# Asking for some first-batch loads in pieces with 1024-byte packets

## The chip, the cores and the metric

The kernel runs on one core of one Trainium2 chip. The metric is the device time of one execution in microseconds (us), lower is better. The engines named below are PE (TensorE, the matmuls), DVE (VectorE), ACT (ScalarE), POOL (GpSimd) and SP (SyncE, which here only issues transfers). Transfers of all issuing engines run on the same 16 DMA engines.

## The reference

There are 8 batches of 3008 rows. Each goes through a gated attention without softmax and then through an MLP mixer over rows (tokens) and over columns (channels). Cut to what is computed:

```python
# u, v: (8, 3008, 256); z: (8, 3008, 64); all float32
scores = (1 / S) * z @ z^T                 # S = 3008
out    = maximum(scores, 0)**2 @ v
x      = u * out                           # the gate
h      = maximum(x^T @ w_tok1, 0) @ w_tok2 # w_tok1 (3008, 256), w_tok2 (256, 3008)
u2     = x + h^T
result = u2 + maximum(u2 @ w_ch1, 0) @ w_ch2   # w_ch1 (256, 1536), w_ch2 (1536, 256)
```

## The kernel before, in words

**Tiling.** The 3008 rows of a batch are cut into six groups of 512 (the last has 448). A group is four tiles of 128 rows (`GK = 4`); the last has three and a tail of 64 rows. `b` counts batches, `q` a group of queries, `g` a group of keys. For each (b, q) the scores with every key group go to PSUM (line 440), ACT takes the relu (L478, L466), DVE squares it (L486, L518), and PE multiplies it with v (L593 in the very first block, L677 elsewhere). At the end of a block, `gate` (L835, and L840 for the odd 64 columns) multiplies the sum with the transposed u, `uT`, on DVE. The gated x goes through a DMA transpose (`turn_x`, L855) to `x_sb`. When all six groups of a batch are there, the mixer of this batch runs: first token product (L900), second (L927), first channel product (L977), second channel product (L1096, in a form with seven products for eight, which uses the precomputed weight sums `w_sums`, L1616 to L1619 on DVE).

**Order of the work.** The program that builds the kernel holds a small model of the engines with costs in us. It decides in which order the pieces are written to each engine's queue (`next_op`, `next_piece`, the main loop at the end). Each engine executes its queue strictly in that order and waits on semaphores where data are missing. A load tells this model its cost through `loading(LOAD)`.

**Loads.** All float32 inputs except the first z are loaded by POOL with a cast to bf16 on the way. `load_v` (L211, and L214 for the tail), `load_u` (L223, L226), `load_w_tok1` (L241, L245), `load_w_tok2` (L251) and `load_w_ch` (L258 for the first channel weight in two parts, L263 for the second in two parts) each issue one transfer per group or part. `rows_of` lays a group out so that a partition takes n consecutive rows (n = 4, or 3 in the last group): for v, u and w_tok1 a partition's piece in SBUF is 4 x 256 bf16 = 2048 bytes, or 1536 in the last group; for a part of w_ch1 it is 1536 bf16 = 3072 bytes; for w_tok2 it is 512 bf16 = 1024 bytes.

In batch 0 POOL is asked for: v of batch 0; u of groups 0 to 3 of batch 0; z of batch 1; and then the list `items`, spread over the steps of batch 0: v of batch 1, w_tok1, w_tok2, w_ch1 and w_ch2, u of the first two groups of batch 1; u of groups 4 and 5 of batch 0 come in between. Nothing but free buffers and the transfers' own semaphores holds POOL back in this stretch. These semaphores are eight lanes used in turn: each POOL transfer waits until the one eight before it has landed, so at most eight are in flight. A group of u is named by m = 6 b + q below.

**Transposes.** SP issues, in one queue, the DMA transposes of u (`turn_u`, L233), of z for the next batch (`turn_z`, L140 and L144), of x (L855), of squared scores that serve a mirrored block (`flip`, L546 and L530), of u2 (L958), and the stores of the result (L1151). An SP transfer that waits, or that cannot be handed over, holds back all behind it.

Of the kernel before, what the change touches and what calls it, by code (L numbers as in the profile page):

```python
# [13 lines left out]
P = 128  # L14
QW = 512
GK = 4
# [41 lines left out]
def kernel(  # L58
# [11 lines left out]
    nc = tc.nc  # L70
# [3 lines left out]
    d_ch = moe_w_ch1.shape[-1]  # L74
# [6 lines left out]
    NQ = (S + QW - 1) // QW  # L81
# [16 lines left out]
    w_tok1_sb = consts.tile([P, KT, d_tok], BF16)  # L98
    w_tok2_sb = consts.tile([P, DT, S], BF16)
    w_ch1_sb = consts.tile([P, DT, d_ch], BF16)  # L100
# [12 lines left out]
    def rows_of(ap, c):  # L113

        n = full_tiles[c]
        return ap[c * QW:c * QW + n * P, :].rearrange("(p t) d -> p t d", t=n)

    def last_rows(ap):
        return ap[(KT - 1) * P:, :]
# [75 lines left out]
    def fill(n, bank):  # L195

        for _ in range(n):
            nc.tensor.matmul(  # L198
                bank, zero[:, :P], zero[:], start=True, stop=True, skip_group_check=True)

    def load_v(b, c):
        if b == 0:

            vt = sb.tile([P, GK, D], BF16, tag="fl", name="v_sb", bufs=ROOM["fl"])
            live["fl"] += 1
            fl_free.pop(0)
        else:
            vt = sb.tile([P, GK, D], BF16, tag="v", name="v_sb", bufs=ROOM["v"])
            live["v"] += 1
        n = full_tiles[c]  # L210
        nc.gpsimd.dma_start(out=vt[:, :n, :], in_=rows_of(v[b], c))  # L211
        if n < GK:
            for r in range(2):
                nc.gpsimd.dma_start(  # L214
                    out=vt[r * TAIL:(r + 1) * TAIL, n, :], in_=last_rows(v[b]))
        vs[b, c] = vt
        v_in[b, c] = Done(pe[0] + 9.0 if b > 1 else 0.0)
        loading(LOAD)

    def load_u(b, q):  # L220
        ur = sb.tile([P, QW // P, D], BF16, tag="ur", name="ur", bufs=4)
        n = full_tiles[q]
        nc.gpsimd.dma_start(out=ur[:, :n, :], in_=rows_of(u[b], q))  # L223
        if n < QW // P:
            nc.gpsimd.memset(ur[TAIL:, n, :], 0.0)
            nc.gpsimd.dma_start(out=ur[:TAIL, n, :], in_=last_rows(u[b]))  # L226
        urs[b, q] = ur
        loading(LOAD)
# [9 lines left out]

    def load_w_tok1(c):
        n = full_tiles[c]  # L240
        nc.gpsimd.dma_start(  # L241
            out=w_tok1_sb[:, c * GK:c * GK + n, :], in_=rows_of(moe_w_tok1, c))
        if n < GK:
            nc.gpsimd.memset(w_tok1_sb[TAIL:, KT - 1, :], 0.0)
            nc.gpsimd.dma_start(  # L245
                out=w_tok1_sb[:TAIL, KT - 1, :], in_=last_rows(moe_w_tok1))
        loading(LOAD)
# [7 lines left out]

    def load_w_ch(part):
        if part < 2:
            nc.gpsimd.dma_start(  # L258
                out=w_ch1_sb[:, part, :], in_=moe_w_ch1[part * P:(part + 1) * P, :])
        else:  # L260
            h = CHT // 2
            c0 = (part - 2) * h
            nc.gpsimd.dma_start(  # L263
                out=w_ch2_sb[:, c0:c0 + h, :],
                in_=moe_w_ch2.rearrange("(cc c) d -> c cc d", c=P)[:, c0:c0 + h, :])
        loading(LOAD * 1.5)
# [46 lines left out]
    def loading(us):  # L313
        loads[0] = max(loads[0], pe[0] + 1.0) + us
# [96 lines left out]
    def can_score(first_unit, most):  # L411

        n, at = 0, live["at"]
        for (b, q, g), pr in units[first_unit:first_unit + most]:
            if (b, q) not in turned or (b, g) not in turned:
                break
            at += pr == 0
            if at > ROOM["at"]:
                break
            n += 1  # L420
        return n
# [1038 lines left out]
    make_identity(nc, ident)  # L1460
    zf0 = [first_z(c) for c in range(NG)]
    load_v(0, 0)
    nc.gpsimd.memset(zs[:, 0, :], 0.0)
    nc.gpsimd.memset(zs[:, KT + 1, :], 0.0)
# [41 lines left out]
    def u_then_turn(m):  # L1506
        load_u(m // NQ, m % NQ)
        later.append((pe[0] + 11.0, lambda: gated[0] >= m - 2,
                      lambda: turn_u(m // NQ, m % NQ)))
# [6 lines left out]
    def when_taken(b, c):  # L1516
        ask(lambda: load_v(b + 1, c),
            lambda: x_done[b, NQ - 1].t is not None and has_room(("v",)))
# [13 lines left out]
    for b in range(B):  # L1532
        base = b * NQ * NG
        for q in range(NQ):
            m = b * NQ + q + 2
            if b == 0:
                if m < NQ:
                    at_group(U_LOADS[m], lambda m=m: load_u(m // NQ, m % NQ))
                late_turn = NQ * NG + 1 + 4 * (m - NQ) if m >= NQ else U_TURNS[m]
                at_group(base + late_turn, lambda m=m: turn_u(m // NQ, m % NQ))  # L1540
            elif m < 2 * NQ:
                at_group(base + q * NG + 2, lambda m=m: ask(lambda: u_then_turn(m)))
        if b == 0:
            at_group(base + 4, lambda b=b: new_zT(b + 1))
            for j in range(NG):
                at_group(base + 4 + j // 3, lambda b=b, j=j: load_z(b + 1, j))
            for half in range(2):
                at_group(base + 9 + 6 * half, lambda b=b, half=half: turn_next_z(b, half))
        else:
            if b == 1:  # L1550
                ask_z(2, base + NG - 1)
            if b + 1 < B:
                last, m = base + NQ * NG - 1, (b + 1) * NQ
                for k in range(3):
                    ask_u(m + k, last)
                if b + 2 < B:
                    ask_z(b + 2, last)
                for c in vorder:
                    at_group(last, lambda b=b, c=c: when_taken(b, c))
                for k in range(3, NQ):  # L1560
                    ask_u(m + k, last)
# [45 lines left out]
    def ask_w_ch(part):  # L1607
        load_w_ch(part)
        w_done[part].t = pe[0] + 16.0
        if part == 3:  # L1610
            push("dve", pe[0] + 18.0, 2.4, 2.5, sum_weights, done=sums_done)
# [12 lines left out]
    def ask_w_tok2(c):  # L1624
        load_w_tok2(c)
        tok2_done[c].t = pe[0] + 10.0

    items = [lambda c=c: load_v(1, c) for c in vorder]
    items += [lambda c=c: load_w_tok1(c) for c in range(NG)]
    items += [lambda c=c: ask_w_tok2(c) for c in range(NG)]  # L1630
    items += [lambda part=part: ask_w_ch(part) for part in range(4)]
    items += [lambda m=m: load_u(m // NQ, m % NQ) for m in (NQ, NQ + 1)]
    for k, item in enumerate(items):
        at_group(NG + 1 + k * (NQ * NG - 2 * NG + W_LATER) // len(items), item)
# [39 lines left out]
    while cur[0] is not None or heads or tails:  # L1674
        run_engines(pe[0])
        ask_some()
        t = pe[0]
# [16 lines left out]
        n = can_score(done_units, most)  # L1694
# [118 lines left out]
```

## Time and profile before

| what | us |
|---|---|
| time, median of 3 runs | 1117.28 (1116.62 to 1120.8) |
| the profiled execution's own time | 1116.15 |
| its span in the profile | 1114.4 |
| PE busy in the span | 1104.5 (99%) |
| DVE busy | 760.5 (68%) |
| ACT busy | 670.5 (60%) |
| POOL busy | 150.6 (14%) |
| packets of POOL's transfers (queue q0) | 27344 packets, 32.32 MB |
| packets of SP's and ACT's transfers (queue q1) | 445024 packets, 131.57 MB |

Busy times are unions of an engine's instructions. Issuing a transfer is not counted as busy. The profiled execution's own time is its span and 1.75 us around it, and lies 1.13 us below the median of the runs. The granted PE clock is 1.0 throughout.

### The profile page before, as it was taken

To read this page: it belongs to the slowest core of one execution; us is meant where nothing else is said; L and a number is where in the kernel's file an instruction comes from. 1 tells how busy PE (TensorE), PEld (TensorE's weight loads), DVE (VectorE), ACT (ScalarE), POOL (GpSimd) and SP (SyncE) were. 2 spreads that over 40 slices of the span, in tenths; PEclk is the share of its full clock that TensorE was granted. 3 is DMA by queue.
4 is the path that set the end of the run, shared out by engine and by line. 5 is a ranking of instruction groups with operands and counts; after the bars stand their busy time and mean duration, and the time that the engine had idled before them with its cause. 6 is when DMAs were issued, how large, how long until landed. Compare 5 with 4: busy or idle time off the path is not lost.

```text
span 1114.4 us, 26494 instructions
## 1 busy us (share of the span) xinstructions
PE 1104.5 (99%) x10714; PEld 672.0 (60%) x10788; DVE 760.5 (68%) x1593; ACT 670.5 (60%) x846; POOL 150.6 (14%) x387
## 2 busy tenths in 40 slices
PE   9999999999999999999999999999999999999998
PEld 3555655766447665676545765567654576545676
DVE  7887866676756866568656676666756677655676
ACT  8996675545755467555666455664566636743464
POOL 5401000221002210022100221002210021000000
PEclk9999999999999999999999999999999999999999
DMA  9999687997859988599794997869987697574222
GB/s 185 192 152 166 134 170 120 174 186 150 162 116 192 169 137 170 99 206 172 141 177 99 210 150 153 163 94 207 162 165 160 115 193 150 119 154 83 66 65 79
DMA packets 473004, 165.98 MB, mean 149 GB/s; under 512 B 435824, under 2 KB 451504, under 8 KB 472880
## 3 DMA queue, kind: packets, MB, share of 16 engines
q1 hardware_dynamic: 445024, 131.57, 60.4%
q0 software_dynamic: 27344, 32.32, 20.8%
q8 instruction: 84, 1.38, 0.5%
q10 hardware_dynamic: 512, 0.38, 0.1%
q14 instruction: 40, 0.33, 0.1%
HBM read 65.40 MB, written 24.64 MB: 81 GB/s over the span
## 4 chain that ended last, share of the span: by engine, by line
PE 98%; DMA 0%; issue 0%; DVE 0%; ACT 0%
PE acc L677 41%; PE hp L977 22%; PE f L1096 18%; PE sc L440 6%; PE a_ps L900 4%; PE h_ps L927 4%; PE f L1209 1%; PE first_acc L593 1%; DMA at<-at 0%; PE op L1255 0%; PE wp L198 0%; DVE cp L811 0%; PE first_acc L198 0%; DVE at L486 0%; PE zp L177 0%
## 5 line engine op out<-in xcount | busy, mean ns | idle before, releaser
L1024 ACT ACTIVATE h2pre<-hp 128x1024 bf16<-128x1024 f32 (+1 forms) x287 | 283.0, 1005 | 227.0 <-PE hp L977 202.0
L677 PEld LDWEIGHTS <-v_sb 64*128 64x128 bf16 x4418 | 235.5, 94 | 223.4 <-issue 1.5
L677 PE MATMUL acc<-at,v_sb 64*128 64x512 bf16 (+1 forms) x2738 | 337.4, 374 | 0.3 <-DMA at<-at 0.3
L478 ACT ACTIVATE at<-sc 128x1024 bf16<-128x1024 f32 (+1 forms) x284 | 279.6, 1029 | 69.6 <-PE sc L440 64.3
L977 PE MATMUL hp<-xT,w_ch_sb 128*128 128x512 bf16 (+1 forms) x1090 | 278.4, 374 | 3.3
L486 DVE TENSOR_TENSOR at<-at 128x1024 bf16<-128x1024 bf16 (+1 forms) x284 | 193.9, 687 | 120.4 <-ACT at L478 118.5
L1096 PEld LDWEIGHTS <-h2pre 128*128 128x128 bf16 x3654 | 225.0, 98 | 55.3 <-issue 2.6
L677 PE MATMUL acc<-fl,v_sb 64*128 64x512 bf16 (+1 forms) x1680 | 192.2, 367 | 0.0
L1096 PE MATMUL f<-w_sums,h2pre 128*128 128x128 bf16 x2088 | 184.5, 219 | 0.1
L977 PEld LDWEIGHTS <-w_ch_sb 128*128 128x128 bf16 x1152 | 104.3, 98 | 82.1 <-issue 0.8
L440 PE MATMUL sc<-zT 64*128 64x512 bf16 (+1 forms) x732 | 131.5, 358 | 0.3 <-ACT zT L1641 0.3
L1096 PE MATMUL f<-w_ch_sb,h2pre 128*128 128x128 bf16 x1566 | 128.5, 219 | 0.0
L811 DVE TENSOR_TENSOR cp<-acc,cp 128x512 f32<-128x512 f32 (+1 forms) x94 | 63.5, 676 | 59.9 <-ACT cp L805 59.0
L805 ACT COPY cp<-acc 128x512 f32<-128x512 f32 (+1 forms) x91 | 53.0, 583 | 81.9 <-PE acc L677 81.4
L466 ACT ACTIVATE at<-sc 128x512 bf16<-128x512 f32 (+3 forms) x164 | 59.1, 452 | 35.9 <-PE sc L440 35.6
L1049 DVE TENSOR_TENSOR h2pre<-h2pre 128x512 bf16<-128x512 bf16 (+1 forms) x141 | 56.4, 400 | 19.0 <-PE f L1096 18.0
L440 PEld LDWEIGHTS <-zT 64*128 64x128 bf16 x732 | 40.4, 94 | 41.7 <-issue 3.5
L1170 DVE TENSOR_TENSOR res<-f,res 128x512 f32<-128x512 f32 (+1 forms) x47 | 30.6, 651 | 49.7 <-PE f L1096 49.7
L1051 DVE TENSOR_TENSOR h2pre<-h2pre 128x512 bf16<-128x512 bf16 (+1 forms) x141 | 57.4, 407 | 9.4 <-PE hp L977 0.5
L936 DVE TENSOR_TENSOR xT<-xT,h_ps 128x1024 bf16<-128x1024 bf16 (+1 forms) x48 | 55.8, 1171 | 11.2 <-PE h_ps L927 11.1
L835 DVE TENSOR_TENSOR xT<-cp,uT 128x512 bf16<-128x512 f32 (+1 forms) x94 | 62.4, 664 | 1.2
L518 DVE TENSOR_TENSOR at<-at 128x512 bf16<-128x512 bf16 (+3 forms) x164 | 43.9, 320 | 25.5 <-ACT at L466 24.3
(80 smaller groups left out, 618.9 us busy)
## 6 DMA issues: line engine op xcount, KB each, us to landing
out_dram<-res SPq DMA_DIRECT2D x80, 256.0 KB, 2.6
v_sb<-in_v_dram POOLq DMA_DIRECT2D x40, 256.0 KB, 4.9
ur<-in_u_dram POOLq DMA_DIRECT2D x40, 256.0 KB, 5.3
out_dram<-res SPq DMA_DIRECT2D x24, 128.0 KB, 2.5
w_tok_sb<-in_moe_w_tok_dram POOLq DMA_DIRECT2D x10, 256.0 KB, 10.5
zs<-in_z_dram POOLq DMA_DIRECT2D x35, 64.0 KB, 3.9
at<-at SPq DMA_TRANSPOSE x123, 2.3
fl<-at SPq DMA_TRANSPOSE x105, 4.7
```

The source lines that it names most:

```text
L440: nc.tensor.matmul(sc[:, r, c0:c1], zT[h, k:k + P], zT[h, m + c0:m + c1], start=True, stop=True)
L466: nc.scalar.activation(a3[:, i, c0:c1], sc[:, r, c0:c1], ACT.Relu, scale=inv_S)
L478: nc.scalar.activation(view, sv, ACT.Relu, scale=inv_S)
L486: nc.vector.tensor_mul(view, view, view)
L677: nc.tensor.matmul(o, vs[blk.b, g][rows, i, dh * P:(dh + 1) * P], rhs, start=(dh, h) not in blk.begun, stop=stop, skip_group_check=True)
L811: nc.vector.tensor_add(cp[:, :W], acc[:, 0, :W], cp[:, :W])
L835: nc.vector.tensor_mul(xT[:, dh, :full * P].rearrange("p (t s) -> p t s", s=P), acc[:, :full * P].rearrange("p (t s) -> p t s", s=P), uT[: ...
L977: nc.tensor.matmul(hp[:, r, :W], w_ch1_sb[:, dc, cc * P:(cc + 1) * P], xT[:, dc, :W], start=(dc == 0), stop=(dc == DT - 1))
L1024: nc.scalar.activation(h2[:, :, :W], hp[:, :, :W], ACT.Relu)
L1049: (3, lambda: nc.vector.tensor_sub(a11, a11, a21)),
L1051: (2, lambda: nc.vector.tensor_sub(a22, a22, a11)),
L1096: banked(nc.tensor.matmul(to[:, j, :], lhs[:, j * P:(j + 1) * P], rhs, start=m in (1, 2) and c2 == 0 and j == 0, stop=c2 == CHT // 2 - 1, ...
```

## The change

Some of the loads that are asked for during batch 0 become two or three transfers each, so that a partition's piece in one transfer is 1024 bytes (512 where a single tile is left over). A new helper, `load_tiles`, issues a group in steps of `by` tiles; with `by = GK` it issues one transfer as before. Split in two are: all six groups of v of batch 1; u of m = 2 to 7; all six groups of w_tok1. Each of the two parts of w_ch1 becomes three transfers of 512 columns. Not touched: v and u of later batches, v of batch 0, u of m = 0 and 1, w_tok2, w_ch2, z and all tails. The planning model is told the same costs as before (the `loading` calls are unchanged). The order of instructions on PE, DVE, ACT and SP is the same in both kernels; POOL has 22 transfers more: 6 for v, 6 for u, 6 for w_tok1 and 4 for w_ch1.

```diff
+    def load_tiles(out, rows, n, by):
+
+        for t in range(0, n, by):
+            tiles = slice(t, min(t + by, n))
+            nc.gpsimd.dma_start(out=out[:, tiles, :], in_=rows[:, tiles, :])
+
     def load_v(b, c):
...
-        nc.gpsimd.dma_start(out=vt[:, :n, :], in_=rows_of(v[b], c))
+        load_tiles(vt, rows_of(v[b], c), n, 2 if b == 1 else GK)
...
     def load_u(b, q):
...
-        nc.gpsimd.dma_start(out=ur[:, :n, :], in_=rows_of(u[b], q))
+        load_tiles(ur, rows_of(u[b], q), n, 2 if 1 < b * NQ + q < NQ + 2 else GK)
...
     def load_w_tok1(c):
         n = full_tiles[c]
-        nc.gpsimd.dma_start(
-            out=w_tok1_sb[:, c * GK:c * GK + n, :], in_=rows_of(moe_w_tok1, c))
+        load_tiles(w_tok1_sb[:, c * GK:c * GK + n, :], rows_of(moe_w_tok1, c), n, 2)
...
     def load_w_ch(part):
         if part < 2:
-            nc.gpsimd.dma_start(
-                out=w_ch1_sb[:, part, :], in_=moe_w_ch1[part * P:(part + 1) * P, :])
+            for c in range(0, d_ch, QW):
+                nc.gpsimd.dma_start(
+                    out=w_ch1_sb[:, part, c:c + QW],
+                    in_=moe_w_ch1[part * P:(part + 1) * P, c:c + QW])
```

## The prediction

> **What bounds the kernel now.** First the page, for the busy shares and the queues.
>
> ```profile
> span 1114.4 us, 26494 instructions
> ...
> PE 1104.5 (99%) x10714; PEld 672.0 (60%) x10788; DVE 760.5 (68%) x1593; ACT 670.5 (60%) x846; POOL 150.6 (14%) x387
> ...
> q1 hardware_dynamic: 445024, 131.57, 60.4%
> q0 software_dynamic: 27344, 32.32, 20.8%
> ```
>
> PE is idle for 1114.4 - 1104.5 = 9.9 us in all. q0 holds POOL's loads, q1 the transposes and stores. Second, the busy time by stretches of 20 us (after the stretch: its length, then PE, PEld, DVE, ACT and POOL, the granted clock, the DMA share and GB/s), to see whether PE waits where the change acts.
>
> ```profile
> 0.00:20.00 20.00, 18.39 (x101) 7.45 (x103) 12.99 (x23) 15.70 (x18) 11.26 (x28) 1.00 0.99 181
> 20.00:40.00 20.00, 19.95 (x174) 10.02 (x175) 17.52 (x27) 19.67 (x24) 12.24 (x24) 1.00 1.20 195
> 40.00:60.00 20.00, 20.00 (x188) 10.95 (x186) 16.81 (x26) 19.02 (x21) 6.88 (x11) 1.00 1.20 193
> 60.00:80.00 20.00, 20.00 (x198) 11.05 (x194) 17.24 (x29) 17.37 (x22) 0.00 (x0) 1.00 1.15 166
> 80.00:100.00 20.00, 19.97 (x193) 11.32 (x189) 16.98 (x33) 18.50 (x24) 2.14 (x6) 1.00 0.83 141
> 100.00:120.00 20.00, 19.86 (x146) 12.10 (x146) 13.60 (x23) 9.43 (x11) 4.03 (x10) 1.00 0.95 174
> ```
>
> From 20 to 120 us PE idles for 0.05 + 0 + 0 + 0.03 + 0.14 = 0.22 us. In the same stretch the DMA engines are full (share 1.15 to 1.20 from 20 to 80, above 1 since packets overlap). The chip is short of DMA there, and PE does not feel it. A busy PE can hide slow matmuls, so I also looked at the chain of waits: it runs its pairs of 512-column matmuls in 1.73 us for 16 both at 48 and 73 us and, with no loads of this kind about, at 156 us.
>
> Third, the queues in single stretches, 30 to 40, 60 to 70 and 70 to 80 us: packets, MB, share.
>
> ```profile
> q0 software_dynamic: 1014, 1.67, 93.9%
> q1 hardware_dynamic: 1013, 0.25, 19.6%
> ...
> q0 software_dynamic: 1822, 1.29, 89.4%
> q1 hardware_dynamic: 1816, 0.45, 44.7%
> ...
> q1 hardware_dynamic: 6201, 1.53, 93.8%
> q0 software_dynamic: 22, 0.01, 0.7%
> ```
>
> Where both queues have work they take turns packet by packet: 1014 to 1013, and 1822 to 1816 although the load packets are then smaller. A transpose packet (0.25 MB / 1013 = 247 bytes) waits behind a load packet each time; alone, six times as many pass. Fourth, the timelines of SP, POOL and DVE, for what that does and who needs it when (start, duration, engine, line).
>
> ```profile
> 29.87 17.97 SPq L140 DMA_TRANSPOSE zT<-zs  x2
> 47.94 9.52 SPq L855 DMA_TRANSPOSE x_sb<-xT  x1
> 57.57 3.35 SPq L233 DMA_TRANSPOSE uT<-ur  x1
> ...
> 85.78 1.43 SPq L233 DMA_TRANSPOSE uT<-ur  x1
> ...
> 35.43 0.53 POOL L241 DMA_DIRECT2D w_tok_sb<-in_moe_w_tok_dram  x1 [1.00 <-DMA v_sb<-in_v_dram]
> ...
> 53.53 0.54 POOL L223 DMA_DIRECT2D ur<-in_u_dram  x1 [1.88 <-DMA w_tok_sb<-in_moe_w_tok_dram]
> ...
> 75.53 0.69 DVE L835 TENSOR_TENSOR xT<-cp,uT 128x512 bf16<-128x512 f32 x1
> ...
> 93.60 0.55 DVE L1616 TENSOR_TENSOR w_sums<-w_ch_sb 128x768 bf16<-128x768 bf16 x1
> ```
>
> SP is stuck for up to 18 us handing over two transposes that take 1.2 us each later on. POOL does not issue freely either: from 28 us on it waits before nearly every load for an earlier one to land.
>
> **The change, part by part.**
>
> *22 more issues on POOL.* A load of a group takes 0.53 us to issue (the 35.43 line), and one of z with a quarter of the elements takes 0.53 too, so half a load costs the same: 22 x 0.53 = 11.7 us more of POOL. Its idle time ahead of the loads from 28.3 to 53.5 us adds up to 12.6 us (each of these is a wait for a landing), and to another 6 us from 10 to 22 us. So the issues mostly fit into waits. If that cover were gone, the last load would come 11.7 us later.
>
> *Smaller packets.* The split transfers of v, u and w_tok1 move 5 x 256 + 192 = 1472 KB each and w_ch1 768 KB, together 5.3 MB in bf16. Per 10 us of all engines, 2 KB packets move 1.67 / 0.939 = 1.78 MB (30 to 40 us), a mix with half in 1 KB packets 1.63 / 0.925 = 1.76 (40 to 50 us, by the same view), 512-byte packets 1.29 / 0.894 = 1.44. So the 5.3 MB, worth 5.3 / 1.78 x 10 = 30 us, grow by 1% to 19%: 0.3 to 6 us. I take 3 us, between the mixed row and the 512-byte row and nearer to the former. The engines are full, so the last load, issued at 53.53 and landing about 17 us later, lands at 74 in place of 71; with none of the issue time hidden and the dear packets, at 71 + 11.7 + 6 = 89.
>
> *Half as much in flight.* Eight transfers of 128 KB in place of eight of 256 KB. At the 160 KB that q0 moves per us (1.67 MB in 10 us) these are 6.4 us of work, above the shortest landing of a small z load, 2.4 us. The engines don't run dry, so nothing is lost.
>
> *Transposes get more turns.* In the v, u, w_tok1 and w_ch1 stretch each load's bytes now give twice (w_ch1: three times) as many turns to q1. The 18 us and 9.5 us on SP should shrink towards half, and the transposes of z, x and u land several us earlier. Gain on PE: at most the 0.22 us above, and with the small gaps up to 240 us (0.78 us in the same view) 1.0 us. I take 0, since no PE wait in that view's stretches ends on one of these transposes.
>
> *Who needs the loads.* Second channel weight: lands by 49.42 + 18.4 = 67.8, first used at 93.60, slack 26 us. First token weight: lands by 47, PE needs it at 98.79, 51 us. First channel weight: by 61, needed at 106.85, 46 us. v of batch 1: by 35, not needed before 88. u of m = 6: lands at 69, SP turns it at 85.78, slack 16 us; m = 7: 71 and 95.83. A delay of 3 us harms none. The delay of 18 us would hit only m = 6, by 2 us on SP, whose product is needed at 98.6. The tightest deadline is a transpose: uT of m = 4, issued at 57.57, lands 13.6 us later at 71.2 and is gated at 75.53 (slack 4.4 us). It should come earlier.
>
> Sum: 1116.15 - 0 + 0 = 1116.15 for the profiled execution. The median of the runs before lies 1.13 us above it, so **1117.3 us**.
>
> **The rivals.**
>
> *Faster, since the transposes are freed.* All PE idle from 20 to 240 us, 1.0 us, is the most that can go: 1116.3. To beat 0.5% (5.6 us, about what a measurement here can tell from no change) it would have to take over half of the 9.9 us, and of these 1.6 lie before 20 us and 4.3 in the last 114 us, out of reach. For: SP's stuck 18 us. Against: PE 20.00 of 20.00.
>
> *Slower, loads late.* The price of a transfer is then its whole landing, one after the other: 22 x 2.4 = 53 us. u of m = 6 lands at 122, uT 4.6 us later, the gate that needs it at 98.6 waits 28 us: 1145. It decides from a delay of about 16 us on, where SP's turn of m = 6 starts to wait. Against: POOL's lines show eight in flight, and z loads landing a few tenths of a us apart. The Trainium skill, DMA: Bandwidth & Descriptors, section Anatomy of one DMA, gives some 2.0 us fixed for each transfer beside its bytes, and its Rules for kernel authors ask to coalesce; taken serially that estimate is 44 us and past that point. The trace agrees with it as a latency (2.4 us), but not as a cost per transfer where eight overlap.
>
> *Slower, by uT of m = 4.* If the transposes get no more turns and all of batch 0's traffic shifts by the 11.7 us of issues, this uT lands at 82.9, 7.4 us after its gate. DVE stands still, and PE with it once the scores in hand are used up: up to 7 us, 1124. It decides from a shift of 4.4 us on. Against: packet for packet turns at two packet sizes. The Trainium skill, same page, section SWDGE vs HWDGE vs iDMA, has the engine change queues only at packets of up to 4096 bytes made of several descriptors; two 1 KB rows in one such packet would give the transposes no more turns. The counts of 1014 to 1013 with 2 KB and 1822 to 1816 with 512-byte packets speak against this.
>
> *The change does not do what it says* (rows joined again): nothing but 11.7 us of POOL, hidden: 1117.3. Against: w_tok2, laid out in 1024-byte pieces, counts more packets per MB (1362 for 1.63 MB at 40 to 50 us).
>
> **How the numbers follow.** No effect on PE 0.88; packets unchanged 0.03, the same time; faster 0.03; loads late 0.03; uT late 0.03. Of the faster case I count 0.02 as over 0.5%, for what no view shows; of the two slower 0.04. So faster 0.02, same 0.94, slower 0.04. The range reaches from the profiled execution's 1116.15 less the 1.0 us of PE idle and less the 0.7 us by which the lowest run lies under the median, 1114.5, to the highest run before, 1120.8.
>
> **What would show it.** L205 in place of L211, L223 and L241, with 22 more loads. q0 with about 1920 + 384 + 2 x 256 = 2800 more packets (1920 of 2048 bytes and 384 of 1536 become two, 256 of 3072 three) plus some for completion: over 30,100. q1's count from 30 to 40 us well above 1013. SP's 17.97 for two turns of z under 12. The last u load of the 53.53 line issued near 64 and landing at 72 to 77. PE idle from 20 to 120 us still under 0.5 us. Wrong it would be if PE showed a gap before L835's block near 75 us, or at 98 us.

## The result and the profile after

The kernel is slower: 1129.45 us (median of 6 runs, 1121.93 to 1132.57) against 1116.95 us (6 runs, 1115.75 to 1120.8), ratio 1.0103, 95% interval 1.0068 to 1.0139. The prediction, 1117.3 us and no change, was wrong. The profiled execution took 1129.5 us, 13.35 us more than that of before.

First the page of the changed kernel: span, busy shares, the two queues, and the shares of the chain that ended last.

```profile
span 1127.7 us, 26591 instructions
PE 1110.6 (98%) x10788; PEld 673.0 (60%) x10788; DVE 760.9 (67%) x1593; ACT 670.9 (59%) x846; POOL 162.3 (14%) x409
q1 hardware_dynamic: 445024, 131.57, 61.1%
q0 software_dynamic: 30512, 32.32, 21.6%
PE 91%; DMA 6%; POOL 1%; ACT 1%; issue 1%; DVE 0%; SPq 0%; POOLq 0%; ACTq 0%
```

The bytes are the same, q0 has 3168 packets more, and POOL's 11.7 us are the 22 issues. The chain now runs through DMA for 6%. The stretches of 20 us (after the stretch: length, PE, PEld, DVE, ACT, POOL, granted clock, DMA share, GB/s) say where:

```profile
20.00:40.00 20.00, 20.00 (x176) 10.09 (x176) 17.57 (x27) 19.67 (x23) 13.00 (x25) 1.00 1.35 175
40.00:60.00 20.00, 20.00 (x188) 11.02 (x186) 16.60 (x26) 19.02 (x22) 8.98 (x17) 1.00 1.34 140
60.00:80.00 20.00, 20.00 (x198) 11.14 (x194) 17.45 (x29) 17.37 (x22) 4.84 (x9) 1.00 1.40 121
80.00:100.00 20.00, 16.45 (x160) 9.09 (x155) 13.66 (x27) 13.45 (x18) 5.12 (x11) 1.00 1.35 165
100.00:120.00 20.00, 14.27 (x88) 8.11 (x88) 8.23 (x11) 6.29 (x9) 1.42 (x4) 0.74 1.15 197
```

PE loses time in one place only, from 96 to 112 us. But the cause begins over 50 us earlier: from 40 to 80 us the DMA engines move 140 and 121 GB/s, where they moved 193 and 166 before, while their busy share is higher (1.34 and 1.40 for 1.20 and 1.15). The timeline of POOL shows what the loads do (start, duration, engine, line, and in brackets the wait before it):

```profile
37.87 0.53 POOL L205 DMA_DIRECT2D w_tok_sb<-in_moe_w_tok_dram  x1 [0.96 <-DMA v_sb<-in_v_dram]
45.49 1.58 POOL L205 DMA_DIRECT2D w_tok_sb<-in_moe_w_tok_dram  x3 [7.09 <-DMA v_sb<-in_v_dram]
...
85.76 1.05 POOL L205 DMA_DIRECT2D ur<-in_u_dram  x2 [2.85 <-DMA w_ch_sb<-in_moe_w_ch_dram]
```

At 37.87 us POOL has eight transfers under way, of 128 KB for the most part, and waits 7.09 us for one to land. The last two of u are issued at 85.76 (the last load was issued at 53.53 before); u of m = 7 lands at 99.5 us, not 70.7, and the second channel weight at 95.8, not 67.8. The chain of waits goes on from there:

```profile
82.37 15.52 DMA ur<-in_u_dram
...
97.94 1.23 SPq L239
...
99.27 5.24 DMA fl<-at
...
104.62 1.03 ACT at L485
...
105.69 0.61 PE sc L447 x2
```

SP's turn of u of m = 6 (L239) waits until 97.94. Behind it in SP's queue stands a transpose of squared scores (`fl<-at`, L553), which was issued at 87.31 before and is now at 99.27. Until it has read its buffer, ACT can't write new scores, and PE has none to use. From the timeline, ACT and then PE:

```profile
104.62 1.94 ACT L485 ACTIVATE at<-sc 128x1024 bf16<-128x1024 f32 x2 [10.55 <-DMA fl<-at]
105.69 0.61 PE L447 MATMUL sc<-zT 64*128 64x512 bf16 x2 [9.21 <-ACT at L485]
```

Matched instruction by instruction, PE is 9.4 us behind the kernel before at the end of this gap and 11.5 us at 112 us; the 2.1 us between are the granted clock, on the mean 0.62 from 106 to 112 us, where it was 1.00. From there to its last matmul the distance stays at 11.4 to 11.5 us. The rest of the 13.35 us, 1.95, comes after the last matmul, whose start was 4.35 us ahead of the end of the span and is now 6.30 ahead. What ends the program is POOL's closing drain; by line (engine, operation, number, then ns as min/median/max), first in the kernel before, then in the changed one:

```profile
L1808 POOLq DRAIN  x3: 45/102/7917, 1105.7 to 1114.1; - x3
```

```profile
L1815 POOLq DRAIN  x3: 45/93/9877, 1117.1 to 1127.5; - x3
```

It begins 4.36 us before the last matmul starts in both and takes 9.88 us, not 7.92; 0.8 us behind its end the span ends, in both.

### The profile page after: what moved, and what is told of

It reads as the page before. It is cut to its first block, busy times and chain, and to the rows that moved or that the text cites. A ratio compares the mean times of both kernels' runs of the same rounds, so it can differ in the third digit from the quotient of the medians.

```text
span 1127.7 us, 26591 instructions
## 1 busy us (share of the span) xinstructions
PE 1110.6 (98%) x10788; PEld 673.0 (60%) x10788; DVE 760.9 (67%) x1593; ACT 670.9 (59%) x846; POOL 162.3 (14%) x409
## 3 DMA queue, kind: packets, MB, share of 16 engines
q0 software_dynamic: 30512, 32.32, 21.6%
## 4 chain that ended last, share of the span: by engine, by line
PE 91%; DMA 6%; POOL 1%; ACT 1%; issue 1%; DVE 0%; SPq 0%; POOLq 0%; ACTq 0%
PE acc L684 36%; PE hp L984 22%; PE f L1103 18%; PE sc L447 5%; PE a_ps L907 4%; PE h_ps L934 4%; DMA w_tok_sb<-in_moe_w_tok_dram 3%; DMA ur<-in_u_dram 1%; PE f L1216 1%; DMA v_sb<-in_v_dram 1%; PE first_acc L600 1%; ACT at L485 1%; DMA at<-at 0%; PE op L1262 0%; DMA fl<-at 0%
## 5 line engine op out<-in xcount | busy, mean ns | idle before, releaser
L984 PE MATMUL hp<-xT,w_ch_sb 128*128 128x512 bf16 (+1 forms) x1152 | 281.7, 375 | 0.0
L943 DVE TENSOR_TENSOR xT<-xT,h_ps 128x1024 bf16<-128x1024 bf16 (+1 forms) x48 | 55.8, 1172 | 11.7 <-PE h_ps L934 11.7
```

What stands on the lines that cost most here:

```text
L984: nc.tensor.matmul(hp[:, r, :W], w_ch1_sb[:, dc, cc * P:(cc + 1) * P], xT[:, dc, :W], start=(dc == 0), stop=(dc == DT - 1))
```

## The experiments

There are two losses to explain, 11.4 us in PE's gap and 1.95 us at the end. For the first, theory A (later expectations call it only the theory): the queue of POOL holds eight transfers, so halved transfers halve the bytes under way, and beside the transposes that is too little to keep the DMA engines at their rate. Rivals: the smaller packets themselves slow the loads; or the rate hardly matters, and it is the lateness of u of m = 6 in SP's queue. In the table, "loads end" is the landing of the last load of this stretch in the profiled execution, PE's gaps are those over 1.5 us from start to start up to 120 us, and "drain" is POOL's closing one. The median of the kernel before lay between 1116.28 and 1116.95 us each time that it was measured beside these.

| kernel | profiled, us | loads end, us | PE gaps, us | drain, us | median, us (range) | ratio, 95% interval |
|---|---|---|---|---|---|---|
| before | 1116.15 | 70.7 | none | 7.92 | | |
| after | 1129.5 | 99.5 | 9.6 | 9.88 | 1129.45 (1121.93 to 1132.57) | 1.0068 to 1.0139 |
| four_in_flight | 1142.62 | 115.3 | 24.4 | 7.92 | 1139.59 (1131.76 to 1147.95) | 1.0150 to 1.0266 |
| six_in_flight | 1127.14 | 92.1 | 6.9, 1.6 | 7.92 | 1117.07 (1115.92 to 1128.94) | 1.0000 to 1.0067 |
| half_partitions | 1130.57 | 99.2 | 4.2, 4.7 | 8.08 | 1124.24 (1118.22 to 1133.23) | 1.0037 to 1.0105 |
| spread | 1123.22 | 80.1 | none | 9.22 | 1124.42 (1123.22 to 1126.06) | 1.0057 to 1.0087 |
| spread_w | 1117.12 | 78.5 | none | 8.73 | 1117.63 (1116.36 to 1121.58) | 1.0003 to 1.0023 |
| split_vu | 1126.67 | 92.5 | 4.2, 2.0 | 9.06 | 1126.01 (1118.0 to 1131.5) | 1.0029 to 1.0104 |
| split_w | 1124.99 | 93.0 | 5.8 | 8.82 | 1117.67 (1116.91 to 1132.31) | 1.0013 to 1.0077 |
| urgent_first | 1131.01 | 99.1 | 10.0 | 9.88 | 1128.36 (1121.66 to 1133.41) | 1.0059 to 1.0146 |
| after_few_turns | 1117.87 | 65.8 | none | 9.88 | 1118.52 (1117.87 to 1119.14) | 1.0008 to 1.0029 |
| before_few_turns | 1116.31 | 63.2 | none | 7.92 | | |
| joined | 1117.69 | 77.2 | none | 7.84 | 1117.27 (1115.88 to 1117.98) | 0.9996 to 1.0014 |
| late_split | 1118.01 | 71.8 | none | 9.88 | 1118.47 (1117.56 to 1128.16) | 1.0006 to 1.0045 |
| w_tok2_pairs | 1115.16 | 69.4 | none | 7.43 | 1116.21 (1115.16 to 1116.65) | 0.9984 to 1.0001 |

Take the drain's share off, and leave aside spread, whose loss lies elsewhere, and the two kernels with work left out: the profiled time follows the end of the loads. Up to 78.5 us it is 1116 to 1118 us, from 92 us on 1124 to 1130, at 115 us 1143.

**Fewer transfers in flight, nothing else changed (four_in_flight).** The kernel before, with whole transfers and 2 KB packets; ahead of each load of the stretch POOL reads a column of the load four places back:

```diff
+    def at_most_four(column):
+        if len(flight) >= 4:
+            after(flight[-4])
+        flight.append(column)
...
+        at_most_four(w_tok1_sb[:, c * GK, :1])
         nc.gpsimd.dma_start(
             out=w_tok1_sb[:, c * GK:c * GK + n, :], in_=rows_of(moe_w_tok1, c))
```

> The kernel before (packets of 2048 and 3072 bytes, whole transfers), but POOL waits before each load of the first batch's list until the load four before it has landed: four transfers of 256 KB in flight, so 1 MB, as the changed kernel has with eight of 128 KB. Theory A (too few bytes in flight: engines that are ahead run dry while one lags, since a lane is free only when all 16 engines are done): the last u load lands after 85 us in place of 70.7, and the time is 1121 to 1135 us. Theory B (packet size: transposes get more turns against small load packets): packets are as before, so the last load lands by 76 and the time is 1116 to 1118 us.

Measured: slower than the change itself, with a median beyond the 1135 us that theory A had as its upper end; the loads end at 115.3 us. Its timeline of PE, and its stretches of 20 us:

```profile
120.97 0.61 PE L456 MATMUL sc<-zT 64*128 64x512 bf16 x2 [24.02 <-ACT at L494]
```

```profile
40.00:60.00 20.00, 20.00 (x188) 11.04 (x186) 16.86 (x27) 18.97 (x22) 4.49 (x11) 1.00 1.26 101
60.00:80.00 20.00, 20.00 (x198) 11.07 (x194) 17.23 (x29) 17.37 (x22) 7.04 (x16) 1.00 1.34 116
```

The same gap at the same block of scores, 24 us long, and the same picture ahead of it: 101 and 116 GB/s at a busy share of 1.26 and 1.34. Depth alone makes it, at the old packets. It goes further than the change probably because here the loads that the change left whole (w_tok2, w_ch2) are held to four as well.

**Smaller transfers with the old packets (half_partitions).** The split of the change, but by partitions:

```diff
+    def load_halves(out, rows):
+        for r in (slice(0, P // 2), slice(P // 2, P)):
+            nc.gpsimd.dma_start(out=out[r], in_=rows[r])
...
-        nc.gpsimd.dma_start(out=vt[:, :n, :], in_=rows_of(v[b], c))
+        if b == 1:
+            load_halves(vt[:, :n, :], rows_of(v[b], c))
...
```

> The same loads split in two as in the change, but by partitions (0 to 63, 64 to 127) and not along a partition, so the packets keep 2048, 1536 and 3072 bytes; 20 transfers more than before, 128 KB each. Theory A (bytes in flight): the last u load lands after 85 us, time 1121 to 1135 us. Theory B (packet size): the last load lands by 76 us, time 1116 to 1118 us. Third theory (POOL's extra issues of 0.53 us): the load phase is 10.6 us longer at most, 82 us, time under 1119 us.

Measured: the loads end at 99.2 us, as in the change (99.5), and PE loses 4.2 and 4.7 us at 90 and 104 us. So packets of 2 KB don't help as long as the transfers are small. POOL's extra issues alone (the third theory) were to end the loads by 82 us and don't explain it. Three of the nine runs lie below theory A's 1121 us; the lowest, 1118.2, is still above what theory B allowed. The Trainium skill, DMA: Bandwidth & Descriptors, Rules for kernel authors, says of two transfers to disjoint partition halves "Don't bother"; the runs agree and put a price on it, 7.9 us of 1116.3.

**Smaller packets in the old transfers (spread, then spread_w).** In spread, v of batch 1, w_tok1 and w_ch1 get 32 bytes of padding in SBUF after every 1024, so that one transfer of 256 KB can't have its rows joined. In spread_w there is no padding: the halves of two groups of w_tok1 are interleaved in SBUF, and w_ch1 is laid out by its three column blocks.

```diff
-    w_ch1_sb = consts.tile([P, DT, d_ch], BF16)
+    w_ch1_sb = consts.tile([P, d_ch // QW, DT, QW], BF16)
...
+        places = w_tok1_sb.rearrange(
+            "p (j h g t) d -> p j g h (t d)", h=2, g=2, t=2)[:, c // 2, c % 2]
+        nc.gpsimd.dma_start(
+            out=places, in_=rows_of(moe_w_tok1, c).rearrange("p (h t) d -> p h (t d)", h=2))
```

> Whole transfers of 256 KB with packets of 1024 bytes: v of batch 1, first token weight and first channel weight are laid out in SBUF with 32 bytes free after every 1024, so a packet ends there (the last group of three tiles goes as 1024 and 512 bytes in two transfers); u is loaded as before. 72% of the changed bytes have the small packets, and 2 MB stay in flight. Theory A (bytes in flight): the last u load lands by 77 us, time 1116 to 1118 us. Theory B (packet size): it lands after 85 us, time 1120 to 1132 us.

> The kernel before with w_tok1 and w_ch1 alone in packets of 1024 B, but in whole transfers of 256 and 384 KB: the places of the two halves in SBUF are kept apart by another group's half, with no padding, so that rows can't be joined; one more transfer for the last group. It has the packets of split_w (two outcomes, 1117.0 to 1117.7 and 1125 to 1132) without its smaller transfers. Bytes in flight (theory): last u lands by 78, no PE gap near 90 to 100 us, 1116 to 1118 us in all runs. Packet size (rival): the two outcomes of split_w again, median 1117.7 or more with single runs over 1124.

Measured: in both the loads end 8 to 9 us later than before (80.1 and 78.5 us for 70.7), and PE does not feel it; the stretches of spread_w:

```profile
60.00:80.00 20.00, 20.00 (x197) 10.98 (x195) 17.25 (x29) 17.37 (x21) 0.62 (x2) 1.00 1.32 168
80.00:100.00 20.00, 19.97 (x193) 11.28 (x190) 16.93 (x32) 18.79 (x25) 2.14 (x6) 1.00 1.01 186
```

So the packets have a price of their own in the loads, and it is hidden. spread_w is slower by 0.13% (1.5 us), of which 0.8 us are the drain (8.73 for 7.92). Three of its ten runs lie over the 1118 us forecast for all, none over 1124. spread nevertheless lost 7 to 8 us, which I had not expected: 1.3 us are its drain, and for the rest PE stops for 0.8 to 1.5 us (from start to start) once in each of six later stretches (at 173, 316, 455, 591, 866 and 989 us), where none of the loads in question is under way; matched instruction by instruction, PE is 0.03 us behind the kernel before at 159 us and 5.75 at its last weight load. So the median of spread, 1124.42, lies where theory B had it, but not by theory B's way, and the loads end between the two forecasts (77 and 85 us). The padding, which spread_w does without, changes where buffers lie in SBUF for the whole run; whether that is the cause was not tried.

**The dose (six_in_flight).** As four_in_flight, with six.

> The kernel before with its whole transfers of 256 KB and packets of 2048 B, where POOL waits so that at most six of the loads of this stretch are under way. Bytes in flight set the load rate (theory): between before (no limit but the queue's eight) and four_in_flight (1139.6 us, last u at 114): last u lands at 76 to 100 us and the time is 1117 to 1130 us, with runs scattered. Packet size sets it (rival): packets are as before, so last u by 72 and 1116 to 1118 us.

Measured: two outcomes. Six of the ten runs took 1115.9 to 1117.4 us, four took 1127.0 to 1128.9, and none lay between. The profile caught one of the late ones: loads end at 92.1 us. Its timeline (POOL, then PE), and the queues from 45 to 55 us (packets, MB, share of 16 engines):

```profile
55.53 0.55 POOL L123 CAST mark<-w_tok_sb 128x1 f32<-128x1 bf16 x1 [11.12 <-DMA w_tok_sb<-in_moe_w_tok_dram]
...
84.08 0.56 PE L456 MATMUL sc<-zT 64*128 64x448 bf16 x2 [6.57 <-DVE cp L827]
```

```profile
q1 hardware_dynamic: 1150, 0.29, 80.2%
q0 software_dynamic: 573, 0.77, 64.7%
```

POOL waited 11.12 us for one transfer, with old packets and whole transfers. The median hides this: at six transfers of 256 KB the kernel stands on the edge, at four all four runs are past it. The four late ones, and loads that end at 92.1 us, speak against the rival (packets as before, so loads by 72 us and 1116 to 1118 in all runs); four_in_flight, late in all its runs, excludes it.

**One half of the change at a time.** split_vu keeps the split of v and u, split_w that of w_tok1 and w_ch1.

Against the changed kernel, the first pair of lines is split_vu (w_ch1 whole again as well), the second pair split_w (u whole again as well).

```diff
-        load_tiles(w_tok1_sb[:, c * GK:c * GK + n, :], rows_of(moe_w_tok1, c), n, 2)
+        load_tiles(w_tok1_sb[:, c * GK:c * GK + n, :], rows_of(moe_w_tok1, c), n, GK)
...
-        load_tiles(vt, rows_of(v[b], c), n, 2 if b == 1 else GK)
+        load_tiles(vt, rows_of(v[b], c), n, GK)
```

> Only v of batch 1 and u of m = 2 to 7 are split as in the change (12 transfers more); first token weight and first channel weight go whole. If the loss grows with the number of bytes that go with little in flight, the last u load lands between 78 and 92 us and PE's gap at 96 us is 0 to 5 us: 1117 to 1123 us. If any stretch of small transfers sets off the whole delay: over 95 us and over 1124 us.

> Only the first token weight and the first channel weight are split as in the change (10 transfers more); v and u go whole. As for the run before: last u load at 76 to 90 us and 1117 to 1122 us if the parts add up; over 95 us and over 1124 us if any stretch sets off the whole delay.

Measured: either half is enough to lose time, but not in every run. Neither of the two forecasts fits: the loads of the profiled, late executions end at 92.5 and 93.0 us, later than if the parts added up (92 and 90 at most) and earlier than the whole delay (over 95), and times over 1124 us come and go from run to run. split_vu has four of six runs over 1126 us and two at 1118.0 and 1119.3; split_w has six runs at 1116.9 to 1117.7, which is its longer drain (0.9 us) and no more, and four at 1125.0 to 1132.3. In the profiled execution of split_w the gap has another cause than in the change. SP's timeline, then PE's:

```profile
74.83 8.46 SPq L239 DMA_TRANSPOSE uT<-ur  x1
83.38 9.86 SPq L862 DMA_TRANSPOSE x_sb<-xT  x2
```

```profile
94.97 0.61 PE L447 MATMUL sc<-zT 64*128 64x512 bf16 x2 [5.45 <-DVE cp L818]
```

The transpose of u of m = 5 took 8.46 us to be handed over and landed at 93.6; its gate on DVE was late, and PE with it. So the loads need not be late for their own readers: it is enough that they are still under way while a transpose is needed.

**The order of the loads (urgent_first).** The changed kernel, with w_ch2 and u of m = 6 and 7 loaded right after w_tok1 and ahead of w_tok2 and w_ch1:

```diff
+    queue = [lambda part=part: load_w_ch(part) for part in (2, 3)]
+    queue += [lambda m=m: load_u(m // NQ, m % NQ) for m in (NQ, NQ + 1)]
+    queue += [lambda c=c: load_w_tok2(c) for c in range(NG)]
+    queue += [lambda part=part: load_w_ch(part) for part in range(2)]
...
```

> The changed kernel with the same transfers in another order on POOL: second channel weight and u of m = 6 and 7 directly behind the first token weight, then second token weight and first channel weight. The orders on PE, DVE, ACT and SP are the same. If the 13 us are lost only because u of m = 6 comes after SP has reached its transpose (and not because the transfers disturb the engines), u of m = 6 lands by 85 us, PE's gap of 9.6 us at 96 us is gone, and the time is 1116 to 1119 us though the load phase still ends near 100 us. If the crowded DMA engines cost PE time in another way, the time stays above 1124 us.

Measured: u of m = 6 and 7 landed by 82 us, and the gap stayed, 10.0 us. My expectation failed here. SP's timeline shows why:

```profile
84.41 6.18 SPq L553 DMA_TRANSPOSE fl<-at  x1
90.69 9.23 SPq L239 DMA_TRANSPOSE uT<-ur  x1
100.02 3.13 SPq L553 DMA_TRANSPOSE fl<-at  x1
```

SP no longer waits for u, but the hand-over of the first `fl<-at` takes 6.18 us and that of u 9.23 us (1.32 and 1.43 before), because w_tok2 (until 94 us) and w_ch1 (until 99 us) are now what is still loading. The next `fl<-at` is issued at 100.02, no earlier than in the change (99.27). Which load is late doesn't matter; that loads run beside the transposes after 84 us does.

**Without the transposes (after_few_turns, before_few_turns).** From both kernels the same 12 transposes of the stretch are left out: z of batch 1, u of m = 3 to 5 and x of groups 1 to 4 of batch 0; buffers turned earlier are read in their place.

```diff
     def turn_u(b, q):
...
+        if b == 0 and q > 2:
+            uTs[b, q] = uTs[0, 0]
+            on_sp(1.25)
+            return
```

> The changed kernel with 12 DMA transposes of the first 85 us left out: those of z of batch 1 (batch 1 uses batch 0's z instead), of u of m = 3 to 5 (they use m = 0's) and of x of groups 1 to 4 of batch 0 (they use group 0's). The output is another one; all matmuls and loads stay. If eight transfers of 128 KB in flight are too few by themselves (a landing takes longer than the engines need for 1 MB), the last u load still lands after 85 us. If it is the transposes between them that make the 16 engines drift apart, so that lanes wait for the slowest, the last u load lands by 72 us, and PE's gap at 96 us is gone, so the time is 1114 to 1119 us.

> The kernel before with the same 12 transposes left out, as the measure for the run above: the last u load lands at 60 to 66 us in place of 70.7 and the time is 1114 to 1118 us, under either reading.

Measured: the loads of the changed kernel now end at 65.8 us, 2.6 after those of before_few_turns (63.2). POOL's timeline and the queue from 40 to 50 us:

```profile
37.44 4.24 POOL L205 DMA_DIRECT2D w_tok_sb<-in_moe_w_tok_dram  x8 [0.90 <-DMA v_sb<-in_v_dram]
```

```profile
q0 software_dynamic: 1959, 1.73, 115.8%
```

Eight transfers go out without a wait between them, 0.53 us apart, and 1.73 MB land in 10 us, more than the 1.63 of the kernel before with its transposes. Small transfers and small packets feed the engines well as long as no transposes run beside them. Of the slowdown 2.1 us are left. In the trace they are the drain: the last matmul starts at 1109.75 us, 0.2 us earlier than in before_few_turns, and the span ends 1.7 us later.

**More in flight (joined).** The kernel before with w_tok1's first four groups in two transfers of 512 KB and each channel weight in one of 768 KB:

```diff
+                out=w_tok1_sb[:, c * GK:(c + 2) * GK, :].rearrange("p (c t) d -> p c (t d)", c=2),
+                in_=moe_w_tok1[c * QW:(c + 2) * QW].rearrange("(c p t) d -> p c (t d)", c=2, t=GK))
...
+                out=w_ch1_sb[:], in_=moe_w_ch1.rearrange("(k p) d -> p k d", p=P))
```

> The kernel before with larger transfers in place of smaller ones, packets unchanged: the first token weight in two transfers of 512 KB and two for its last groups, each channel weight in one of 768 KB; 4 transfers fewer. Bytes in flight (theory): more of them can't make the load phase longer, so the last u lands by 71 us and all runs lie at 1115.5 to 1118.5 us; it is not faster either, since PE idled 0.22 us from 20 to 120 us before. A large transfer holds back what stands behind it (rival): the last u, issued behind the channel weights, or the transposes of u land later, and PE shows a gap of a few us at 75 to 100 us: 1118 to 1125 us.

Measured: no difference clear of the noise, all 11 runs from 1115.88 to 1117.98 (median 1117.27 against 1116.28). But the loads end at 77.2 us, not by 71, and PE has one wait of 0.77 us at 78.86 that it did not have before: the rival named the right effect, at a fraction of its price. Past eight transfers of 256 KB more bytes in flight bring nothing here.

**The second loss (late_split, w_tok2_pairs).** In the kernels above, the drain went with the packets of q0 alone: 7.92 us in all that have 27344, 9.88 in all that have 30512, whether their loads were late or not. To tell packets from an after-effect of the load phase, late_split adds packets where nothing is tight, and w_tok2_pairs takes some away:

```diff
+        load_tiles(vt, rows_of(v[b], c), n, 2 if b in (4, 5) else GK)
...
+        load_tiles(ur, rows_of(u[b], q), n, 2 if b in (4, 5) else GK)
```

```diff
     def load_w_tok2(c):
-        cols = slice(c * QW, c * QW + widths[c])
...
+        if c % 2 == 0:
+            cols = slice(c * QW, (c + 1) * QW + widths[c + 1])
...
```

> The kernel before with v and u of batches 4 and 5 (not those of the load phase) in two transfers each, 24 transfers and about 3456 packets more on q0. Theory of the end: POOL's closing drain grows with the number of packets that q0 carried, 0.62 ns each by the kernels so far (7.92 us at 27344, 9.88 at 30512), and ends the program; the drain takes 10.0 to 10.2 us, the span between the last matmul and the end is 6.4 to 6.5 us in place of 4.3, the time 1118.2 to 1118.7 us, and PE is not late anywhere before. Rival: the longer end was an after-effect of the disturbed load phase; then the drain stays at 7.9 us, and the time at 1116.3.

> The kernel before with the second token weight in three transfers with pieces of 2048 B (1920 in the last) in place of six with 1024 B: about 816 packets fewer on q0. Theory of the end: the drain takes 7.4 us and the time falls by 0.5 us, to 1115.8, if the load phase stays as it is (as it did with joined). Rival: drain 7.9 us, time 1116.3; or a later end of the loads, 1117 and more.

Measured: by their pages q0 carried 30800 packets in late_split and 26528 in w_tok2_pairs. The drain of the first, then of the second:

```profile
L1814 POOLq DRAIN  x3: 45/102/9878, 1105.5 to 1115.9; - x3
```

```profile
L1809 POOLq DRAIN  x3: 45/93/7428, 1105.2 to 1113.1; - x3
```

late_split is slower by 2.1 us (median 1118.47 against 1116.4), with its last matmul at 1109.89 us, 0.14 us before that of the kernel before: nothing but the drain. Packets make it, wherever they are sent. The transfers alone do not: half_partitions has 20 more of them, but only 320 packets more, and a drain of 8.08 us. The count does not give it to the last step, though: 30800 packets were to take 10.0 to 10.2 us and take the same 9.88 as 30512. In w_tok2_pairs the drain is 0.49 us shorter, as forecast; its median is 0.2 us below that of before (ratio 0.9984 to 1.0001), so a gain is likely and not shown; the 1115.8 us forecast was not reached. It has the lowest median of the versions tried.

## Why the prediction was wrong

By its own steps:

*22 more issues on POOL.* Right as far as it went: 22 x 0.53 = 11.7 us were forecast, POOL's busy time rose by 162.3 - 150.6 = 11.7, and it lay in waits. The forecast of q0's count was right too (over 30,100; it is 30512). But the packets had no price in the sum after they had landed. That is a missing term: 1.95 us in the closing drain, which the page doesn't count as busy. After_few_turns and late_split, with PE on time, show that this term alone is worth 2.1 us.

*Smaller packets.* Half right. 3 us were forecast for the end of the loads, with 18 as the far end; spread_w shows 7.8 us with the weights alone and spread 9.4. It was hidden, as forecast.

*Half as much in flight.* This is the step that failed. I had compared 6.4 us of work under way with the 2.4 us in which a small load lands when little else runs, and concluded that the engines don't run dry and nothing is lost. Without the transposes that is true, as after_few_turns shows. Beside them it is not: with less under way the rate fell to nearly half. The loads ended at 99.5 us in place of my 74. The 2.4 us were the wrong measure: a load of this stretch took far longer to land, and half the bytes landed only a little sooner. On the page of the kernel before, a load of 256 KB of w_tok1 or w_tok2 takes 10.5 us from issue to landing (the last number of this line, a median):

```profile
w_tok_sb<-in_moe_w_tok_dram POOLq DMA_DIRECT2D x10, 256.0 KB, 10.5
```

Halves of 128 KB of w_tok1 take 8.8 us in the changed kernel, and 4.8 us in after_few_turns, without the transposes. Four and six whole transfers in flight show that it is the bytes under way, not their packets, and half_partitions that the new packet size isn't needed for it.

*Transposes get more turns.* Right as far as it went, and then reversed. From 30 to 40 us of the changed kernel (packets, MB, share):

```profile
q0 software_dynamic: 1242, 1.03, 77.4%
q1 hardware_dynamic: 2320, 0.57, 58.3%
```

2320 transpose packets passed, for 1013 before, SP's two turns of z took 5.11 us, not 17.97, and uT of m = 4, which one rival had late, landed at 55.05 us, not 71.2. Later the transposes became slow as well: the two of x at 66.47 us took 14.85 us, for 4.72 before.

*Who needs the loads.* The slack was read rightly: 16 us for u of m = 6 and 26 for w_ch2. The delay was 28 us, so both were late (DVE waited 2.44 us for w_ch2 at 95.91). The place of the gap, 98 us, had been named as a sign of error. What I had left out is that loads on their way also hold up transposes in SP's queue that read none of them; urgent_first shows that this alone makes the whole gap.

*The rival "loads late"* (chance 0.03) was right in kind and in its point of decision: 16 us after 71 is 87, and the kernels divide between 80 and 92. Its mechanism was not: transfers were not served one after the other (22 x 2.4 us, 1145 us); eight overlapped throughout, at a lower rate. The price was 28 us of delay and 11.4 us of time. Here the Trainium skill's rule that I had set against the trace, to coalesce transfers (DMA: Bandwidth & Descriptors, Rules for kernel authors), would have given the right sign; I had turned it down because eight overlap, which is true and did not decide.

*The range.* Its upper end came from the spread of the runs before. The trace of before could not show how the load rate depends on depth, and the step put no bound on it. The lowest rate among its rows would not have been enough: with q0's 1.29 MB of 60 to 70 us in place of the mean of some 1.6 MB per 10 us, 44 us of loading (27 to 71) become 55 and end at 82, short of the 87 at which the time changes. But the 10.5 us of the line above would have: if a load of 128 KB is supposed to take as long as one of 256 KB, eight of them bring 1.05 MB in 10.5 us, which is 1.0 MB in 10 us; the 5.3 MB then take 53 us in place of 30, and the last load lands 23 us later, at 94, past the 87. Such a bound would have put the late case into the range.

## What to carry to other kernels

Where a queue holds a fixed number of transfers, splitting them takes bytes from under way; that loads overlap, or that one alone lands quickly, doesn't say that fewer bytes will do when transposes share the engines. Read the DMA's busy share together with its GB/s: 1.40 at 121 GB/s is a worse state than 1.15 at 166. And when a load phase may run longer, look not only at who reads the loads, but at every transpose that is due while they are still under way. Where POOL's drain is the last thing in a program, each packet that it sent costs some 0.6 ns there, so fewer and larger packets are worth a little even where their transfer is hidden.

## What the runs showed of the hardware

Full engines are not fast engines. From 60 to 70 us of the changed kernel the DMA line shows a 9 in nearly every slice, and the queues read:

```profile
q1 hardware_dynamic: 1424, 0.35, 78.2%
q0 software_dynamic: 664, 0.54, 70.5%
```

A share of 78.2% of 16 engines over 10 us, by 1424 packets, is 88 ns for a transpose packet of 247 bytes, and 70.5% by 664 packets is 170 ns for a load packet. Before, in the same stretch, it was 39 ns (44.7%, 1816 packets) and 79 ns (89.4%, 1822). On the mean a packet took about twice as long, and half as much moved: 0.88 MB for 1.76. The mean hides two kinds, though. In the trace's single records, half of the 419 load packets of 1024 bytes in this stretch took 96 ns or less, and 96 ns is also their median in the kernel before (40 to 50 us); but 108 of the 419 took over 250 ns, where before none of 748 did. So not every packet is slow: some stall. The same slowdown shows in six_in_flight, with 2 KB packets (q1's 80.2% by 1150 packets, 112 ns), so it belongs neither to a packet size nor to the changed kernel. That few bytes under way bring it on is shown by four_in_flight and half_partitions, and that the transposes have to run beside them by the one pair with 12 of them left out; what the stalled packets wait for is not shown, since the trace doesn't say which engine carried a packet. That some engines run ahead and wait for others, which a deeper queue would cover, is only a guess.

The loss comes or stays away from one run to the next, most plainly in six_in_flight (six runs without, four with, 10 us apart). Two runs of late_split, whose load phase is that of the kernel before, took 1124.7 and 1128.2 us, and four of 96 runs of the unchanged kernel 1124.48, 1122.04, 1120.87 and 1120.8. Where the granted clock of these late runs is on record, it lies at 0.996 to 0.998, and at 0.999 or 1.0 in the others of both kernels; behind PE's gap in the changed kernel it was 0.994 in the profiled run. So PE probably had such a gap in them too, and the kernel before stands near this edge itself; no profile caught such a run.

POOL's drain at the end grew from 7.43 us at 26528 packets to 9.88 at 30512: (9.88 - 7.43) / 3984 = 0.6 ns for each, in steps of 82 ns (7.84 us at 27280, 7.92 at 27344), though every packet had landed long before: in the changed kernel the last of q0 ends at 951.4 us, and the drain begins at 1117.1.

PE's gap of 9.2 us also cost clock: the granted clock was 1.00 up to 100 us, 0.50 from 101 to 110 and 1.00 again from 112, so it fell within the gap and stayed low for some 5 us behind its end at 105.7. That cost 2.1 us on top. The stops of up to 1.1 us in spread left it at 1.00.
